# A filter layer and an ELU layer on one core: another opening, and a plain first unit

## The chip, the cores and the metric

The kernel runs on one core of a Trainium2 chip. The core has a matrix engine (PE, with its weight loads PEld), a vector engine (DVE), a scalar engine (ACT), a general one (POOL), a sequencer that issues transfers (SP), and 16 DMA engines that all transfer queues share. SP, ACT and POOL each have a queue; SP's is called q1 in the profile, ACT's q10 and POOL's q0. The metric is device time in microseconds; lower is better. The runs of a kernel spread by about 0.2%.

## What is computed

```python
X = np.fft.rfft(x, axis=1)                 # x: 8 x 3008 x 256
F = (filt_r + 1j * filt_i)[None, :, :]     # 1505 x 256 each
y = np.fft.irfft(X * F, n=3008, axis=1)
h = y.reshape(24064, 256) @ w_in           # 256 x 2048
g = np.where(h > 0, h, np.exp(np.minimum(h, 0)) - 1)
out = g @ w_out                            # 2048 x 256
```

x and the filter are float32. The two weight matrices arrive as float64: `setup_inputs` multiplies them by a float64 scalar. So the kernel has to convert them, 2 x 524288 numbers, before it can use them.

## The kernel before

**Items and quarters.** The output tokens of a batch are cut into 6 units (b, m); a unit has 4 quarters of the hidden width. Quarter q of a unit is one item. PE's order is written out by hand at the end of the kernel: item i interleaves the up steps of item i (`up_steps`, L616: y times a block of w_in, then the ELU) with the down steps of item i - 1 (`down_steps`, L703: g times a block of w_out, summed in PSUM over the four quarters). Up and down both use a seven-product scheme for the 2 x 2 blocks in place of eight products: `w_sums` forms sums of weight blocks, `n_sums` sums of y, and the products feed one another through ACT and DVE. Each step is two matmuls of 128 x 128 by 256 columns (224 in units with m = 0). All other work is hung into this order by a plan: `at(quad, place, fn)` puts a call at a place of item number quad. Numbers below zero are the time ahead of the first item.

**The transform.** 3008 = 47 x 64. For batches 1 to 7, `x_load` reads 4 rows of each half, `a_unit` multiplies with a cosine and sine table, the result goes through DRAM (`z_write`, `z_read`), then `b_unit`, `filtered` (the filter) and `bi_unit`, again through DRAM (`y_write`, `y_read`), and `n_unit` makes the y that an item uses. These steps of batch b + 1 lie between the items of batch b.

**The opening.** Batch 0 can't be hidden behind items, and the weights must be converted, so both share the stretch ahead of the first item, inside the pool "boot":

- `x_load_first` (L300) reads piece c of x, six pieces of two halves each, and a table of the full width `tf`, all on SP. The upper half is 64 rows of 4 KB, the lower half is read in mirrored order, 1 KB at a time.
- `a_first` (L310) is the first matrix step, eight matmuls a piece; ACT copies its PSUM into `zt` (L322).
- `t_first` (L325) transposes a group g of eight (L334), ACT copies (L335). `b_first` (L388) does the second matrix step (L379) and the four products with the filter on DVE (`products`, L383 to L386); `bi_first` (L402) the way back (also L379, ACT copies L411, L412); `y_write_first` writes y to DRAM. `bi_first` runs two groups behind `b_first`.
- The filter is rearranged first by 28 transfers from DRAM to DRAM on POOL (`f_arrange`, L859), then read into `ff` by 16 more (`f_read_first`, L366). Later `f_pairs` (L878) makes a second layout for the other batches, from the rearranged copy.
- The 16 weight pieces k (w_in and w_out, two each for each of the four quarters) are fetched by `w_fetch` (L787) on POOL or SP, and converted in three parts: `w_split` (two masks on DVE, L815, L816), `w_float` (four ACT steps, L825: low word, high mantissa, exponent twice), `w_join` (sign L831, sum L833, product L840 or L846, on DVE). `w_sums` (L857) follows. The temporaries sit in tiles that are idle in the opening.

Pieces 0 to 11 are converted ahead of the first item, 12 to 15 within the first four items. A DMA of the SP queue may wait for the eighth DMA before it, and so on POOL.

Of the kernel before, what the change touches and what calls it, by code (L numbers as in the profile page):

```python
# [23 lines left out]
N1 = 47  # L24
N2 = 64
NF = N // 2 + 1
P = 128
# [14 lines left out]
def _make_tables():  # L42
# [27 lines left out]
    tf = np.ascontiguousarray(ta.reshape(P, H, 4, K2).transpose(0, 1, 3, 2)).reshape(P, H, P)  # L70
# [51 lines left out]
    tw = np.ascontiguousarray(tn[:, 0:8].reshape(4, K2, 8, 2, 2, 32).transpose(1, 0, 2, 4, 3, 5)).reshape(P, 8, P)  # L122
# [19 lines left out]
def kernel(  # L142
# [47 lines left out]
    edges = glob.tile([P, 2], FP32, name="edges")  # L190
    unit = glob.tile([P, P], FP32, name="unit")
    fd = fdp.tile([NG, 2, 48, 2, 2, D], FP32, name="fd")
# [107 lines left out]
    def x_load_first(c):  # L300
        t = xs[0, c]
        u = 1 if c == 0 else 0
        nc.sync.dma_start(t[HALVES[0]].rearrange("p u d -> p (u d)"), raw(x, XC * c, [[N1 * D, 64], [1, XC * D]]))
        nc.sync.dma_start(t[HALVES[1], u:XC, :], raw(x, N1 - XC * c - u, [[N1 * D, 64], [-D, XC - u], [1, D]]))
        if c < 2:
            nc.sync.dma_start(tas[0, c], tf_d[:, 4 * c:4 * c + 4, :])
        elif c % 2 == 0:
            nc.sync.dma_start(tas.pop(("pair", c // 2)), tf_d[:, 4 * c:4 * c + 8, :])
# [16 lines left out]
    def t_first(g):  # L325

        t = t2s[0, g] = t4p.tile([P, 4, D], FP32, tag="t4", name="tf") if g % 4 > 1 else t2[:, g % 4]
        for j in range(2):
            i = j + 2 * (g % 2 if g < 4 else 0)
            ps = psO.tile([P, 2, 256], FP32, tag="po%d" % i, name="po%d" % i)  # L330
            for u in range(2):
                k = 4 * g + 2 * j + u
                for dh in range(2):
                    nc.tensor.transpose(ps[0:ROWS, u, ts(dh, P)], zt[k // 16][dh][:, ts(k % 16, ROWS)], eye)  # L334
            nc.scalar.activation(out=t[0:ROWS, 2 * j:2 * j + 2, :], in_=ps[0:ROWS], func=AXT.Copy)  # L335
# [30 lines left out]
    def f_read_first(g, t):  # L366
        for a, r in enumerate((LO, HI)):
            nc.gpsimd.dma_start(t[r].rearrange("p c u d -> p (c u d)"), fd[g, a].rearrange("q c u d -> q (c u d)"))
# [12 lines left out]
    def products(re, im, f, sr, si, p, q):  # L381

        nc.vector.tensor_tensor(out=sr, in0=re, in1=f[:, 0], op=ALU.mult)  # L383
        nc.vector.tensor_tensor(out=si, in0=re, in1=f[:, 1], op=ALU.mult)
        nc.vector.scalar_tensor_tensor(out=p, in0=im, scalar=-1.0, in1=f[:, 1], op0=ALU.mult, op1=ALU.mult)
        nc.vector.tensor_tensor(out=q, in0=im, in1=f[:, 0], op=ALU.mult)  # L386
# [15 lines left out]
    def bi_first(g):  # L402
        s = ss.pop((0, g))
        t = t3s[0, g] = (t2 if g > 5 else t3f)[:, g % 2]

        pa, pb = (psO.tile([P, 2, 256], FP32, tag="po%d" % i, name="po%d" % i)
                  for i in ((0, 1) if g > 2 and g % 2 else (2, 3)))
        for o, table, sv in ((0, gr, s[0]), (64, gi, s[1])):
            for ps, k in ((pa, LO), (pb, HI)):
                tile_mm(ps[o:o + 64], table, k, sv, g == 0 and k == LO)  # L410
        nc.scalar.activation(out=t[:, 0:2, :], in_=pa, func=AXT.Copy)  # L411
        nc.scalar.activation(out=t[:, 2:4, :], in_=pb, func=AXT.Copy)  # L412
# [113 lines left out]
    def y_read(b, m, *parts):  # L526
        t = t4s[b, m] = t4p.tile([P, 4, D], FP32, tag="t4", name="t4")
        for k in parts or (slice(0, K2),):
            if whole(b, m):
                r = slice(4 * k.start, 4 * k.stop)  # L530
                nc.sync.dma_start(t[r], yds[b].rearrange("k (p i) d -> (k p) i d", p=4)[r, 4 * m:4 * m + 4, :])
                continue
            for r in range(2):
                o = 64 * r
                nc.sync.dma_start(t[o + 2 * k.start:o + 2 * k.stop].rearrange("q i d -> q (i d)"),
                                  yds[b][k.start + r:k.stop:2].rearrange("k (p i) d -> k p (i d)", p=4)
                                  [:, :, 4 * m * D:4 * m * D + 4 * D])
# [9 lines left out]
    def n_whole(b, m):  # L547
# [10 lines left out]
        b11, b12, b21, b22 = rows  # L558
        t = yp.tile([P, 2, 256], FP32, tag="yb", name="yb")[:, :, 0:h]
# [55 lines left out]

    def up_steps(b, m, q):  # L616

# [85 lines left out]
    def down_steps(b, m, q):  # L703
        h = half(m)
# [82 lines left out]
    def w_fetch(k, queue=nc.gpsimd):  # L787
        q, j = divmod(k, 4)

        if k in (3, 4, 14, 15):  # L790
            wd = t2[:, k % 11 - 3].rearrange("p u d -> p (u d)")
        elif k == 10:
            wd = t1p.tile([P, XC, D], FP32, tag="t1", name="wd").rearrange("p u d -> p (u d)")
        elif k in (6, 7, 8, 9):
            wd = xp.tile([P, 2, 2, D], FP32, tag="xc", name="wd").rearrange("p k u d -> p (k u d)")
        else:
            wd = fbufs[{5: 0, 11: 0, 12: 1, 13: 2}.get(k, k)].rearrange("p c u d -> p (c u d)")
# [14 lines left out]
    def w_split(k):  # L812
        m, e, f, l = wts[k] = wtmp[{9: 2, 10: 1, 11: 0, 12: 3, 13: 4, 15: 5}.get(k, k % 2)]
# [4 lines left out]
    def w_float(k, *parts):  # L818
        m, e, f, l = wts[k]
        ef = e.bitcast(FP32)  # L820
        steps = ((l, wds[k][:, :, 0], AXT.Identity, 2.0 ** -52, 0.0), (f, m, AXT.Identity, 2.0 ** -20, 1.0),
                 (ef, e, AXT.Relu, -8.0, edges[:, 0:1]), (e, ef, AXT.Relu, -1.0, edges[:, 1:2]))
        for i in parts or range(4):
# [3 lines left out]
    def w_join(k, parts=(0, 1)):  # L827
        q, j = divmod(k, 4)
        m, e, f, l = wts[k]
        if 0 in parts:  # L830
            nc.vector.scalar_tensor_tensor(out=e, in0=wds.pop(k)[:, :, 1], scalar=0x80000000, in1=e,  # L831
                                           op0=ALU.bitwise_and, op1=ALU.bitwise_or)
            nc.vector.tensor_tensor(out=f, in0=f, in1=l, op=ALU.add)  # L833
        if 1 not in parts:
            return
        e = e.bitcast(FP32)
# [10 lines left out]
        if j % 2 == 1 and k < 7:  # L847
            w_sums(k)
# [10 lines left out]
    def f_arrange():  # L859

        for c, src in enumerate((filt_r, filt_i)):
            for a in range(2):
                nc.gpsimd.dma_start(fd[:, a, 0:48:2, c, :, :].rearrange("g q u d -> q g (u d)"),
                                    raw(src, 2 * a, [[64 * D, 24], [4 * D, NG], [1, 2 * D]]))
                for u in range(2):
                    g0 = 1 if a == u == 0 else 0
                    for j, n in ((0, 16), (16, 7)):
                        nc.gpsimd.dma_start(fd[g0:NG, a, 1 + 2 * j:2 * (j + n):2, c, u, :].rearrange("g q d -> q g d"),
                                            raw(src, 64 * (j + 1) - 4 * g0 - 2 * a - u,
                                                [[64 * D, n], [-4 * D, NG - g0], [1, D]]))  # L870

                g0 = 0 if a else 1
                nc.gpsimd.dma_start(fd[g0:NG, a, 47, c, :, :].rearrange("g u d -> g (u d)"),
                                    raw(src, 4, [[2 * D, NG - g0], [1, 2 * D]]))
            nc.gpsimd.dma_start(fd[0, 0, 1:48:2, c, 0, :], raw(src, 32, [[64 * D, 24], [1, D]]))
            nc.gpsimd.dma_start(fd[0, 0, 47:48, c, 1, :], raw(src, 4, [[D, 1], [1, D]]))

    def f_pairs(c, u):  # L878

        src = fd.rearrange("g a q c u d -> (g a) q c u d")[:, :, c, u, :]  # L880
        dst = fp.rearrange("g (a u) k c h d -> (g a) u k c h d", u=2)[:, u, :, c, :, :]
        nc.sync.dma_start(dst[:, :, 0, :], src[:, 0:48:2, :])
# [273 lines left out]
```

## Time and profile before

| | us |
|---|---|
| median of 3 runs | 2547.76 (2545.4 to 2550.08) |
| the profiled execution | 2546.68 |
| its span, first to last instruction | 2544.9 |
| first transpose L334 starts | 43.98 |
| first product with the filter L383 starts | 49.74 |
| last product with the filter L386 ends | 75.07 |
| first up product L631 starts | 87.57 |
| first up product of the second unit starts | 136.79 |

The mean granted clock of PE is 0.997. A busy share is an average over the span; in the opening each stage has its own limit, so it is read by stage. The chain of waits goes back from the last instruction to what released it. A float32 matmul leaves two MATMUL records, a transpose one. The length of one record is longer than the distance to the next, since matmuls and DVE or ACT instructions overlap at their ends; where work stands back to back, the distance from start to start is what it costs.

### The profile page before, as it was taken

To read this page: it belongs to the slowest core of one execution; us is meant where nothing else is said; L and a number is where in the kernel's file an instruction comes from. 1 tells how busy PE (TensorE), PEld (TensorE's weight loads), DVE (VectorE), ACT (ScalarE), POOL (GpSimd) and SP (SyncE) were. 2 spreads that over 40 slices of the span, in tenths; PEclk is the share of its full clock that TensorE was granted. 3 is DMA by queue.
4 is the path that set the end of the run, shared out by engine and by line. 5 is a ranking of instruction groups with operands and counts; after the bars stand their busy time and mean duration, and the time that the engine had idled before them with its cause. 6 is when DMAs were issued, how large, how long until landed. Compare 5 with 4: busy or idle time off the path is not lost.

```text
span 2544.9 us, 45370 instructions
## 1 busy us (share of the span) xinstructions
PE 2507.5 (99%) x17266; PEld 2158.4 (85%) x17266; DVE 2119.8 (83%) x3649; ACT 1524.0 (60%) x2680; POOL 156.9 (6%) x315
## 2 busy tenths in 40 slices
PE   6999999999999999999999999999999999999999
PEld 4788889888898888988889888888889888898887
DVE  6978888888888988889888898788897888876766
ACT  6766556655565555665555655656655665555554
POOL 5000100010000000000000000000010001000000
PEclk9999999999999999999999999999999999999999
DMA  9662213523234222342224321343213322111010
GB/s 282 184 182 59 69 39 80 135 59 70 48 93 108 63 67 50 103 97 69 49 52 131 82 67 36 84 110 82 57 48 92 85 51 69 41 41 29 9 28 17
DMA packets 229453, 198.36 MB, mean 78 GB/s; under 512 B 128326, under 2 KB 201558, under 8 KB 229236
## 3 DMA queue, kind: packets, MB, share of 16 engines
q1 hardware_dynamic: 214740, 164.57, 26.4%
q0 software_dynamic: 14000, 30.44, 4.4%
q8 instruction: 136, 2.23, 0.4%
q14 instruction: 81, 0.66, 0.1%
q10 hardware_dynamic: 496, 0.46, 0.1%
HBM read 123.50 MB, written 78.12 MB: 79 GB/s over the span
## 4 chain that ended last, share of the span: by engine, by line
PE 96%; DMA 2%; DVE 1%; ACT 1%; issue 0%; SPq 0%; ACTq 0%; DVEq 0%
PE po L715 45%; PE phs L631 25%; PE phd L631 13%; PE pha L631 6%; PE psn L580 2%; PE pf L434 1%; PE pv L501 1%; DMA xc<-in_x_dram 1%; PE psa L253 1%; PE po L379 1%; DMA x<-in_x_dram 0%; PE po L334 0%; PE psr L379 0%; PE psa L272 0%; DVE g L639 0%
## 5 line engine op out<-in xcount | busy, mean ns | idle before, releaser
L715 PE MATMUL po<-g,wo 128*128 128x256 f32 (+1 forms) x5376 | 1318.5, 377 | 0.0
L715 PEld LDWEIGHTS po<-g,wo 128*128 128x128 f32 x5376 | 1011.9, 190 | 166.0 <-issue 52.4
L642 ACT ACTIVATE g<-phs 128x512 f32<-128x512 f32 (+1 forms) x576 | 338.7, 588 | 749.4 <-PE phs L631 749.2
L649 ACT ACTIVATE e<-e 128x512 f32<-128x512 f32 (+1 forms) x768 | 477.4, 622 | 24.4
L639 DVE TENSOR_TENSOR g<-phd,g 128x512 f32<-128x512 f32 (+1 forms) x384 | 259.4, 676 | 194.4 <-ACT e L649 115.7
L653 DVE SCALAR_TENSOR_TENSOR g<-e,g 128x512 f32<-128x512 f32 (+1 forms) x576 | 387.8, 673 | 14.5 <-ACT e L649 14.4
L631 PE MATMUL phs<-y,wi 128*128 128x256 f32 (+1 forms) x1536 | 387.5, 375 | 0.4 <-ACT y L555 0.4
L631 PE MATMUL phd<-y,wi 128*128 128x256 f32 (+1 forms) x1504 | 379.7, 375 | 0.4 <-DVE g L639 0.4
L648 ACT ACTIVATE e<-g 128x512 f32<-128x512 f32 (+1 forms) x576 | 354.0, 615 | 36.8 <-DVE g L639 29.4
L631 PEld LDWEIGHTS phs<-y,wi 128*128 128x128 f32 x1536 | 291.4, 190 | 33.9 <-ACT y L555 0.6
L631 PEld LDWEIGHTS phd<-y,wi 128*128 128x128 f32 x1504 | 285.2, 190 | 33.7 <-DVE g L639 0.8
L653 DVE SCALAR_TENSOR_TENSOR g<-e,phs 128x512 f32<-128x512 f32 (+1 forms) x192 | 129.8, 676 | 88.4 <-ACT e L649 88.4
L631 PE MATMUL phs<-yt,wi 128*128 128x256 f32 (+1 forms) x768 | 193.9, 375 | 0.9 <-ACT g L642 0.9
L631 PE MATMUL phs<-yb,wi 128*128 128x256 f32 (+1 forms) x768 | 193.8, 375 | 0.6 <-ACT g L642 0.6
L631 PE MATMUL pha<-yb,wi 128*128 128x256 f32 (+1 forms) x736 | 185.9, 375 | 0.0
L648 ACT ACTIVATE e<-phs 128x512 f32<-128x512 f32 (+1 forms) x192 | 112.3, 585 | 116.5 <-PE phs L631 116.5
L373 POOL DMA_DIRECT2D fall<-fp x224 | 110.5, 501 | 822.0 <-DVE r L478 796.4
L631 PEld LDWEIGHTS phs<-yt,wi 128*128 128x128 f32 x768 | 145.7, 190 | 18.0 <-ACT g L642 1.5
L631 PEld LDWEIGHTS phs<-yb,wi 128*128 128x128 f32 x768 | 143.4, 190 | 19.9 <-ACT g L642 1.0
L639 DVE TENSOR_TENSOR g<-pha,g 128x512 f32<-128x512 f32 (+1 forms) x192 | 129.4, 674 | 32.8 <-PE pha L631 32.7
L631 PEld LDWEIGHTS pha<-yb,wi 128*128 128x128 f32 x736 | 139.8, 190 | 16.1
L692 DVE TENSOR_TENSOR g<-g,g 128x512 f32<-128x512 f32 (+1 forms) x192 | 130.7, 681 | 6.7
(190 smaller groups left out, 2067.8 us busy)
## 6 DMA issues: line engine op xcount, KB each, us to landing
yd<-t SPq DMA_DIRECT2D x127, 192.0 KB
t<-yd SPq DMA_DIRECT2D x92, 256.0 KB
fall<-fp POOLq DMA_DIRECT2D x224, 96.0 KB, 2.9
t<-z SPq DMA_DIRECT2D x224, 96.0 KB
out_dram<-o SPq DMA_DIRECT2D x624, 32.0 KB
z<-t SPq DMA_DIRECT2D x144, 128.0 KB
xc<-in_x_dram SPq DMA_DIRECT2D x84, 128.0 KB
xc<-in_x_dram SPq DMA_DIRECT2D x161, 64.0 KB
```

Source lines behind the costliest of these rows:

```text
L253: nc.tensor.matmul(ps[k][1][a:a + 32, u, :], w[r, u, 32 * o:32 * o + 32], parts[o][r, u, :], start=True, stop=True, tile_position=(32 * k, a))
L373: nc.gpsimd.dma_start(t[32 * a:32 * a + 24].rearrange("p c u d -> p (c u d)"), fp[g, a].rearrange("q c u d -> q (c u d)"))
L379: nc.tensor.matmul(ps[:, u:u + w, :], table[k, v, :], r[k, u:u + w, :], start=n == 0, stop=n == len(rhs) - 1)
L580: nc.tensor.matmul(o, t[r, i - 4 * m, ds(dh * P + 64 * c, 64)], w[r, i - 4 * m, :], start=True, stop=True)
L631: nc.tensor.matmul(ps[:, a, 0:h], w_in[q][:, COMBO[n], a, :], y[n], start=start and a == 0, stop=True, skip_group_check=True)
L639: nc.vector.tensor_tensor(out=g[o], in0=i0, in1=i1, op=ALU.add)
L642: nc.scalar.activation(out=g[o], in_=i0, func=AXT.Copy)
L648: nc.scalar.activation(out=e, in_=src, func=AXT.Relu, scale=-1.0)
L649: nc.scalar.activation(out=e, in_=e, func=AXT.Exp, scale=-1.0)
L653: nc.vector.scalar_tensor_tensor(out=g[n], in0=es[n], scalar=1.0, in1=src, op0=ALU.subtract, op1=ALU.max)
L692: nc.vector.tensor_tensor(out=b12, in0=b22, in1=b12, op=ALU.subtract)
L715: nc.tensor.matmul(po[i][:, u, 0:h], w_out[q][:, COMBO[n], a, :], g[n][:, a, :], start=q == 0 and a == 0 and n in (1, 3, 6, 4), stop=True, ...
```

## The change

Five things change, all in the opening and in the first unit (0, 0).

- **x on two queues.** The upper halves of x go on SP, the lower ones on POOL, all twelve transfers at the head of the queues. The table is half as wide (`tf` keeps two of four columns); a new `a_table(c)` spreads it by one copy and two products with a column of signs on DVE. Memsets move: the four of `zt` from POOL to DVE. PE gets warm-up matmuls ahead of and between the pieces.
- **The filter goes straight into SBUF.** `f_first(a, k, parts, queue)` replaces `f_arrange` and `f_read_first`. It fills `ff`, now laid out by frequency, in two halves (k = 0 and 8), mirrored rows on SP, straight and short ones on POOL. `f_pairs` reads the filter itself.
- **`t_first` by plain matmuls** of 64 x 64 blocks with the unit matrix instead of transposes.
- **Plain first unit.** For unit (0, 0) the steps are eight plain block products up and eight down; n_sums isn't called, and no sums of weights are needed until the second unit. These sums move to POOL, at items 1 to 5.
- **Weights piecewise.** `w_float` has three steps (the high mantissa is scaled in the sum on DVE). Pieces 0 to 5 and 7 are converted ahead of the first item; the other nine, cut into split, first and second half of the join, go between the exponential and the maximum of single blocks of items 0 to 3. The lower y writes of groups 0 to 6 go on POOL. Reads of x for batch 1 move from the end of the opening to item 2, and its x_unit, a_unit and z_write come one item later.

The core of the diff:

```diff
-    def x_load_first(c):
+    def x_load_first(c, h):
         t = xs[0, c]
+        if h == 0:
+            nc.sync.dma_start(t[HALVES[0]].rearrange("p u d -> p (u d)"), raw(x, XC * c, [[N1 * D, 64], [1, XC * D]]))
+            return
         u = 1 if c == 0 else 0
-        nc.sync.dma_start(t[HALVES[0]].rearrange("p u d -> p (u d)"), raw(x, XC * c, [[N1 * D, 64], [1, XC * D]]))
-        nc.sync.dma_start(t[HALVES[1], u:XC, :], raw(x, N1 - XC * c - u, [[N1 * D, 64], [-D, XC - u], [1, D]]))
...
+        nc.gpsimd.dma_start(t[HALVES[1], u:XC, :], raw(x, N1 - XC * c - u, [[N1 * D, 64], [-D, XC - u], [1, D]]))
+    def a_table(c):
+        t = th[:, XC * c:XC * c + XC]
+        o = tas[0, c].rearrange("p u (k f) -> p u k f", f=4)
+        nc.vector.tensor_copy(out=o[:, :, :, 0:4:2], in_=t)
+        for f, k in ((1, 1), (3, 0)):
+            nc.vector.tensor_scalar(out=o[:, :, :, f], in0=t[:, :, :, k], scalar1=signs, scalar2=None, op0=ALU.mult)
...
+        for k in range(4):
+            for dh in range(2):
+                for o, n in ((0, 64), (64, ROWS - 64)):
+                    for r, p in zip(HALVES, ps):
+                        nc.tensor.matmul(p[o:o + n, k, dh, :], zt[k // 2][dh][r, (2 * g + k % 2) * ROWS + o:(2 * g + k % 2) * ROWS + o + n],
+                                         eye[r, r], start=True, stop=True)
...
+    def f_first(a, k, parts, queue):
+        o, row, e = 64 * a, 16 * a + k, 1 if a == k == 0 else 0
+        for c, src in enumerate((filt_r, filt_i)):
+            if "f" in parts:
+                queue.dma_start(ff[o:o + 48:2, c, k:k + 8].rearrange("q k d -> q (k d)"), raw(src, row, [[64 * D, 24], [1, 8 * D]]))
+            for j, m, part in ((0, 16, "m"), (16, 7, "s")):
+                if part in parts:
+                    r = o + 1 + 2 * j
+                    queue.dma_start(ff[r:r + 2 * m:2, c, k + e:k + 8], raw(src, 64 * (j + 1) - row - e, [[64 * D, m], [-D, 8 - e], [1, D]]))
...
+    def plain_ups(b, m, q):
...
+        def step(i, j, k):
+            if k == 0:
+                held[i, j] = bank("php")
+            n, ps = held[i, j]
+            for a in range(2):
+                nc.tensor.matmul(ps[:, a, 0:h], w_in[q][:, 2 * k + i, a, :], rows[k][j],
+                                 start=k == a == 0, stop=True, skip_group_check=True)
+            if k == 1:
+                src = ps[:, :, 0:h]
+                e = ep.tile([P, 2, 256], FP32, tag="e", name="e")[:, :, 0:h]
+                nc.scalar.activation(out=e, in_=src, func=AXT.Relu, scale=-1.0)
+                nc.scalar.activation(out=e, in_=e, func=AXT.Exp, scale=-1.0)
+                for fn, a in plan.get((q, 7, i, j), ()):
+                    fn(*a)
+                nc.vector.scalar_tensor_tensor(out=g[i, j], in0=e, scalar=1.0, in1=src, op0=ALU.subtract, op1=ALU.max)
+                banks.append(held.pop((i, j))[0])
+                for fn, a in plan.get((q, 8, i, j), ()):
+                    fn(*a)
...
+            for c in range(NXC):
+                x_load_first(c, 0)
+                x_load_first(c, 1)
+                if c == 0:
+                    nc.gpsimd.dma_start(flat_th[:, 2 * XC:H], tf_d[:, 2 * XC:H])
+            nc.sync.dma_start(once, once_d)
+            w_fetch(0)
+            for k in range(0, 16, 8):
+                for parts, queue in (("m", nc.sync), ("f", nc.gpsimd), ("s", nc.gpsimd)):
+                    for a in range(2):
+                        f_first(a, k, parts, queue)
+                if k == 0:
+                    nc.sync.dma_start(gs, gs_d)
+                    w_fetch(1)
...
+            for c in range(NXC):
+                a_table(c)
+            for c in range(NXC):
+                a_first(c)
+                if c < NXC - 1:
+                    warm(1, 256)
+            for g in range(2):
+                t_first(g)
+            step(0)
+            for g in range(2, 4):
+                t_first(g)
+            w_join(0)
...
+        rest = (8, 6, 9, 10, 11, 12, 13, 14, 15)
+        line = []
+        for n, k in enumerate(rest):
+            line += [(k2, "s") for k2 in rest[n + 1:n + 2]] + [(k, "a"), (k, "b")]
...
+        for quad, *counts in ((0, 1, 1, 1, 1, 1, 1, 1, 0), (1, 1, 1, 1, 1, 1, 1, 1, 1), (2, 1, 1, 1, 1, 1, 1, 1, 1), (3, 1, 1, 1, 0, 0, 0, 0, 0)):
+            for n, count in enumerate(counts):
+                plan.setdefault((quad, 7 + n % 2, *BLOCKS[n // 2]), []).append((convert, (count,)))
```

## The prediction

> **What bounds the kernel now.** The totals and the forty slices come first. PE is busy 99% of the span; the one slice below 9 is the first, and it is also the one in which POOL works and in which the transfers run at 9 tenths of their engines.
>
> ```profile
> span 2544.9 us, 45370 instructions
> PE 2507.5 (99%) x17266; PEld 2158.4 (85%) x17266; DVE 2119.8 (83%) x3649; ACT 1524.0 (60%) x2680; POOL 156.9 (6%) x315
> ...
> PE   6999999999999999999999999999999999999999
> ...
> DMA  9662213523234222342224321343213322111010
> ```
>
> So every change of PE's work after the opening counts in full, and an earlier start of that work counts in full too. Next the chain of waits of the first 90 us: in time order, start, length, what.
>
> ```profile
> 3.20 12.56 DMA xc<-in_x_dram
> 15.78 12.88 DMA xc<-in_x_dram
> 28.68 11.88 DMA x<-in_x_dram
> 40.69 3.46 PE psa L315 x16
> 44.70 3.57 PE po L334 x31
> ```
>
> Until 40.6 the opening hangs on the pieces of x, and on nothing PE does. Third, busy time by stage (columns: PE, PEld, DVE, ACT, POOL, then PE's granted clock, DMA share, GB/s). I cut at the first transpose L334, the end of the filter step, the first up product L631, and the first of the second unit.
>
> ```profile
> 0.00:43.98 43.98, 19.14 (x97) 18.15 (x97) 26.24 (x53) 29.16 (x52) 22.34 (x45) 0.88 1.00 307
> 43.98:76.98 33.00, 32.54 (x270) 18.34 (x268) 27.10 (x50) 25.03 (x47) 11.38 (x20) 1.00 0.94 235
> 76.98:87.57 10.59, 8.30 (x31) 4.44 (x30) 9.49 (x23) 10.00 (x18) 0.00 (x0) 1.00 0.79 238
> 87.57:136.79 49.22, 45.41 (x281) 41.25 (x282) 45.82 (x88) 36.01 (x65) 0.52 (x1) 1.00 0.60 161
> ```
>
> Stage 1 (44 us) is bound by bytes: DMA share 1.00. Stage 2 (33) is shared by PE and DVE. Stage 3 (10.6) is the trip of y through DRAM. Stage 4 is the first unit. The waits of the same stretch show what holds the start of the products:
>
> ```profile
> PE psa L315 <- DMA tn<-tf_t: 16.4, 2, 14.7
> ...
> DVE rq L383 <- DMA ff<-fd: 3.4, 1, 3.4
> ```
>
> **Stage 1, x first.** Before, the queues carry, ahead of the last piece of x, weights 0 to 6, 1.5 MB of table and the filters' copy through DRAM: 44 us at 307 GB/s. After, ahead of it stand on SP a third of the half table and six upper halves, on POOL six lower halves and the rest of the table; the filters, `once` and weight 0 follow. The queues share the engines. In the stretch 6 to 14 us the two rows are:
>
> ```profile
> q0 software_dynamic: 480, 1.54, 66.1%
> q1 hardware_dynamic: 504, 0.79, 36.2%
> ```
>
> Equal counts of packets, not of bytes, though one has 3.2 KB packets and the other 1.6. So POOL's 1600 packets up to its last piece of x (192 + 5 x 256 of 1 KB, 128 of 4 KB) let about 1600 of SP pass: 128 of 2 KB, 384 + 256 of 4 KB (x, two weights), 128 of 1.5 KB, some 700 of 1 KB (`once`, mirrored filters). A packet of about 1.1 KB costs 74 ns of an engine (88 to 94 us: 1030 in 79.6% of 96 engine-us), one of 3.4 KB 196 ns (2 to 6 us: 225 in 69% of 64), so 4 KB about 210, an estimate. Sum 2176 x 0.074 + 768 x 0.21 + 27 = 349 engine-us, over 16 and the overlapped share of 1.04: 21 us. From 3.2 it lands at 24.2. Bounds: only x and table (3.9 MB at 307 GB/s) 16; 60 packets per us of POOL as in 6 to 14, 30. I take 24.2, by rows of just this competition.
>
> Per piece PE needs 2.0 us (L315 x16 at 23.84) and one warm matmul, 0.4: hidden but for the last. The 18 DVE steps that spread the half table (0.3 to 0.4 us each by the 0.42 of L815, estimate 5.5 us in all) come after a 3.5 us memset and end near 13, ahead of the pieces; without that cover they would cost their 0.9 us a piece. The first t_first starts at 24.2 + 2.0 + 0.7 (copies L322) = 26.9, against 43.98.
>
> **Stage 2.** t_first turns one group with 64 records of 64x64 form, where before it took 8 transposes. The nearest row of that form is L580 x128 in 2.05 us, so 1.03 per group, against 1.02 of L334 x8: no gain, no loss. But on ACT weight 0's conversion (3 steps, 0.57 + 0.73 + 0.73 start to start) now stands behind two groups' copies (4 x 0.5), and on DVE its join (three steps, 0.60, 0.60, 0.72 as L831, L833, L840) before the first product: copies end 30.0, float 32.0, join 2.0, first product 34.0, where before it was 49.74 (after the 3.41 wait for `ff`). The filter no longer goes through DRAM: 44 transfers (28 of L863 to L876, 16 of L368) become 26 that write `ff` directly. Its first half, 14 of them behind x on two queues, lands near 29.5 (POOL's last two wait for two slots, then 0.6 us of issue and about 3 to land): covered by 4 us; the second near 34, not needed before 46. From first product to last end: 8 x 4 x 0.60 = 19.2, three splits 2.0, one join 2.0, PE waits 1.5 (before 2.3): 24.7, end 58.7 (before 75.07). POOL now issues seven of the eight lower y writes; 0.6 us each with 3 us between, nothing queued behind waits.
>
> **Stage 3** keeps its length: from the last product 12.5 us to the first up product: 71.2 against 87.57, a gain of 16.3. DVE must do five joins and six splits in it, 5 x 2.0 + 6 x 0.67 = 14, done 1.5 us after that, just ahead of the first g. Bounds 10 to 22 by x alone (at 30 and 18).
>
> **Stage 4, plain first unit.** Eight up and eight down steps a quarter for seven: 8 more steps of 0.757 (L631 from 107.86 to 108.62): +6.06, on PE, certain. Saved on DVE: the four L592 sums, and per quarter some Strassen sums, not on the path. Before, 49 steps (37.1), one psn (1.8) and two psa (3.8) fill 42.7 of the 49.2 us: 6.5 us of stall, the longest behind DVE (1.67 and 0.60 before L631 phd). I let them go, as plain blocks don't feed each other, and the two psa move behind the unit with their own cover. What is late next: nine conversions (8, 6, 9 to 15) go between exp and max of the blocks. ACT has per block 1.12, per conversion 2.03 (one step of 0.62 fewer than before) and, as its exponent steps wait for a split queued behind a max on DVE, 0.65 more: 16 x 1.12 + 9 x 2.68 + 1.1 = 43 us for 56 steps (42.4): even. In order: in the second quarter PE waits for a bank 1.5; weight 13 is joined 37.6 us after the first up product and wanted at 35.2, 2.4; at the unit's end two ACT copies of `po` hold the next down, 0.8 (before they lay under the last steps); x_unit and a_unit of batch 1 come a quad later, which leaves one quad (12.1 us) for psa copies, four z writes (3.5), landing 3.0, reads 1.6 + 2.7, 0.9 ahead: 11.7, so 0.3. The read of y for the second unit now stands on SP behind ten weight transfers; 5.25 MB at some 290 GB/s (82 to 88 us) put it 13 us after the first up product, wanted at 18: covered, by 5 us. Sum 5.0; bounds 0 (all even out) and 11 (each twice over). POOL's 32 sums (L857 0.73 each, 23 us) run beside; they're needed from the fourth quarter on. The pairs' copies now read the filters themselves, and later reads of yd are cut in four for two: SP's issue time, off the path.
>
> **Sum.** -16.3 + 6.06 - 6.5 + 5.0 = -11.7 on the profiled execution's 2546.68 (span 2544.9), which lies 1.1 below the median shown: 2535 by it, 2536 as a median. A measurement of this kernel tells no change from one within 0.2%, 5.1 us.
>
> **Rivals.** (a) x comes sooner, as if bytes alone counted (18 us): 6 us less, 2530. For: the share sometimes exceeds 1.08. Against: the equal packets. (b) x on two queues comes hardly sooner than 30, or PE starts stage 2 at a low clock: before, an idle stretch (25.9 to 30.1) is followed by a granted clock of 0.63 to 0.69 until 45. After, the gap between the first two pieces is about 3.3 us. Price: the last piece 3.46 for 2.0 and some 3 us of stage 2: 2541; with x at 30, 2542. The Trainium skill, "TensorE: Matmul & The Clock Gate", Part 1, has an idle window of about 3.4 us halve the clock, and a busy one restore it; the trace's fall after 4.3 us idle agrees, its 15 us of return doesn't.
> (c) POOL can't issue while DVE works. Before, POOL's issues at 2.4 to 5.3 us lie under the 3.47 us memset of `ff` and take 0.55 as others, against it. If the memsets (1.2 to 6.5) held POOL, its pieces would start 5 us later, partly made up as SP would be done: +4, 2540. The Trainium skill, "SBUF — State Buffer", "SBUF: two separate sides", says that POOL's queue starves under a two-port DVE copy; the six copies of the half table are such, and no run here shows them yet.
> (d) Slower: the conversions pace the first unit. Their 0.65 us hand-over is worked out, not seen; ACT and DVE are in order, so a block's max waits behind a split that waits for a temp, and the temp for a join. It decides when a hand-over costs 1.3 us more in each of nine (11.7); at 2.5 more (22) the time is 2558. For it: ACT has no slack (43 of 42.4). Against: DVE has (about 9 of 12 us a quarter), and four banks let PE run one quarter ahead.
>
> **How the numbers follow.** Forecast 0.52; (a) 0.15; (b) 0.12; (c) 0.08; (d) 0.13. Faster: 0.52 + 0.15, most of (b) and (c): 0.80; within 0.2%: 0.08; slower 0.12. Range 2525 (x at 16 and three of the five us of stall gone) to 2548 (x at 30 and stall 11, or the start of d); without d the forecast's own is 2529 to 2543.
>
> **What would show it.** Last x piece near 24; first t_first near 27 (before 43.98); first product near 34, waiting for weight 0's join and not for `ff`; first up product near 71; 56 steps in some 49 us; no DVE wait of PE before them above 2 us. Wrong if x lands near 30, if the products wait for `ff`, or if PE waits in the first unit add up to 12 us or more.

## The result, and the profile after

The changed kernel takes 2558.1 us (median; 2552.4 to 2560.3), the kernel before 2547.6 (2545.4 to 2550.1) beside it: a ratio of 1.0038, 95% interval 1.0025 to 1.0051. The forecast was 2536, faster. The change costs 10.5 us where 11.7 were to be won.

The profiled execution of the changed kernel is the shortest of its six, 2552.35 us; the other five took 2557 to 2560. So the trace below accounts for 5.7 us of loss against the profiled execution of before, and the rest has to be found elsewhere (the first experiment). Its head, totals and two rows of slices:

```profile
span 2550.5 us, 46325 instructions
...
PE 2520.4 (99%) x17766; PEld 2167.4 (85%) x17766; DVE 2105.0 (83%) x3607; ACT 1509.4 (59%) x2652; POOL 173.0 (7%) x325
...
PE   7899999999999999999999999999999999999999
...
DMA  8653213512234232342224321343223322111010
```

PE is as full as before, its second slice excepted (64 to 127 us), which was 9 before and is 8 now. The stages, cut at the first record of the turn L346, the end of the last copies of the filter step, the first up product L663 and the first of the second unit L730 (busy time of PE, PEld, DVE, ACT, POOL, then PE's granted clock, DMA share, GB/s):

```profile
0.00:23.65 23.65, 18.88 (x114) 14.80 (x114) 9.24 (x29) 12.14 (x24) 10.09 (x20) 1.00 0.94 238
23.65:71.97 48.32, 38.01 (x719) 23.92 (x719) 29.25 (x50) 24.22 (x44) 13.14 (x23) 0.89 0.72 184
71.97:81.32 9.35, 8.46 (x32) 4.36 (x31) 9.07 (x18) 7.87 (x13) 1.09 (x2) 1.00 0.77 232
81.32:136.46 55.14, 49.23 (x276) 46.20 (x277) 47.33 (x78) 37.84 (x66) 23.56 (x26) 1.00 0.53 175
```

Stage 1 is done 20 us sooner than before, 3 sooner than forecast. Stage 2 takes 48.3 us where it took 33.0, and PE is busy for 38 of them. The first up product comes at 81.3: of the 16.3 us that were to be gained, 6.25 are left. The first unit takes 55.1 us, about 6 more than the 49 forecast for its 56 steps. At the second unit's first product, 136.46 against 136.79, only 0.3 is left of the gain.

The chain of waits shows the opening (start, length, what):

```profile
2.10 8.87 DMA t<-tf_t
12.83 2.02 PE psa L322 x16
...
21.94 1.80 PE psa L322 x16
28.93 5.84 issue
40.73 2.71 issue
```

Where the chain of before hung on the pieces of x until 40.6, this one hangs on the table `tf` until 11, and from 12.8 to 23.7 on PE's own work on the pieces of x, 2.2 us each, of which 0.43 is a warm-up matmul. PE waits for no piece of x there. Then the chain holds two pieces called "issue": PE stands still and waits for nothing that the profile shows. The waits of 23 to 72 us (engine, line, waited for: total, times, longest) say what these do:

```profile
PE po L346 <- issue: 9.1, 3, 5.8
...
DVE rq L407 <- PE po L402: 7.0, 3, 4.8
DVE rq L407 <- PE psi L402: 5.9, 2, 5.4
```

The products wait for PE now, 5.4 us before the first and 4.8 before the third, where before they waited 3.4 for `ff`. No product waits for `ff` any more. PE in the first unit, and in the 54 us behind it:

```profile
PE php L663 <- DVE g L672: 4.9, 4, 1.9
PE php L663 <- DVE wi L947: 1.0, 1, 1.0
```

```profile
PE phd L730 <- DVE g L738: 2.0, 1, 2.0
```

So there are three places to explain: PE without work in the turn, DVE late in the first unit, DVE late once more behind it.

### The profile page after: what moved, and what is told of

It reads as the page before. It is cut to its first block, busy times and chain, and to the rows that moved or that the text cites. A ratio compares the mean times of both kernels' runs of the same rounds, so it can differ in the third digit from the quotient of the medians.

```text
span 2550.5 us, 46325 instructions
## 1 busy us (share of the span) xinstructions
PE 2520.4 (99%) x17766; PEld 2167.4 (85%) x17766; DVE 2105.0 (83%) x3607; ACT 1509.4 (59%) x2652; POOL 173.0 (7%) x325
## 4 chain that ended last, share of the span: by engine, by line
PE 95%; DVE 2%; DMA 1%; issue 1%; ACT 1%; SPq 1%; POOL 0%; ACTq 0%; DVEq 0%; POOLq 0%
PE po L816 44%; PE phs L730 25%; PE phd L730 12%; PE pha L730 6%; PE psn L608 2%; PE pf L458 1%; PE pv L525 1%; PE psa L254 1%; PE po L402 1%; PE po L690 0%; SPq L866 0%; PE po L346 0%; PE psa L322 0%; DMA t<-tf_t 0%; PE psr L402 0%
## 5 line engine op out<-in xcount | busy, mean ns | idle before, releaser
L816 PE MATMUL po<-g,wo 128*128 128x256 f32 (+1 forms) x5264 | 1293.8, 377 | 0.0
L816 PEld LDWEIGHTS po<-g,wo 128*128 128x128 f32 x5264 | 990.8, 190 | 165.3 <-issue 51.7
L741 ACT ACTIVATE g<-phs 128x512 f32<-128x512 f32 (+1 forms) x564 | 332.2, 589 | 743.4 <-PE phs L730 743.3
L748 ACT ACTIVATE e<-e 128x512 f32<-128x512 f32 (+1 forms) x752 | 468.1, 623 | 23.9
L752 DVE SCALAR_TENSOR_TENSOR g<-e,g 128x512 f32<-128x512 f32 (+1 forms) x564 | 380.2, 674 | 14.2 <-ACT e L748 14.1
L730 PE MATMUL phs<-y,wi 128*128 128x256 f32 (+1 forms) x1504 | 380.0, 375 | 0.0
L730 PE MATMUL phd<-y,wi 128*128 128x256 f32 (+1 forms) x1488 | 376.0, 375 | 0.4 <-DVE g L738 0.4
L747 ACT ACTIVATE e<-g 128x512 f32<-128x512 f32 (+1 forms) x564 | 347.1, 615 | 36.0 <-DVE g L738 29.2
L730 PEld LDWEIGHTS phs<-y,wi 128*128 128x128 f32 x1504 | 285.6, 190 | 33.0
L730 PEld LDWEIGHTS phd<-y,wi 128*128 128x128 f32 x1488 | 282.2, 190 | 33.7 <-DVE g L738 0.8
L730 PE MATMUL phs<-yb,wi 128*128 128x256 f32 (+1 forms) x752 | 190.2, 375 | 0.3 <-ACT g L741 0.3
L730 PE MATMUL phs<-yt,wi 128*128 128x256 f32 (+1 forms) x752 | 190.0, 375 | 0.0
L730 PE MATMUL pha<-yb,wi 128*128 128x256 f32 (+1 forms) x736 | 185.9, 375 | 0.0
L730 PEld LDWEIGHTS phs<-yb,wi 128*128 128x128 f32 x752 | 140.4, 190 | 19.6 <-ACT g L741 0.7
L730 PEld LDWEIGHTS phs<-yt,wi 128*128 128x128 f32 x752 | 142.8, 190 | 16.5
L730 PEld LDWEIGHTS pha<-yb,wi 128*128 128x128 f32 x736 | 139.8, 190 | 16.1
```

Of the source, the lines that this page charges most:

```text
L730: nc.tensor.matmul(ps[:, a, 0:h], w_in[q][:, COMBO[n], a, :], y[n], start=start and a == 0, stop=True, skip_group_check=True)
L741: nc.scalar.activation(out=g[o], in_=i0, func=AXT.Copy)
L747: nc.scalar.activation(out=e, in_=src, func=AXT.Relu, scale=-1.0)
L748: nc.scalar.activation(out=e, in_=e, func=AXT.Exp, scale=-1.0)
L752: nc.vector.scalar_tensor_tensor(out=g[n], in0=es[n], scalar=1.0, in1=src, op0=ALU.subtract, op1=ALU.max)
L816: nc.tensor.matmul(po[i][:, u, 0:h], w_out[q][:, COMBO[n], a, :], g[n][:, a, :], start=q == 0 and a == 0 and n in (1, 3, 6, 4), stop=True, ...
```

## The experiments

**A second profile of the changed kernel.** No edit.

> The changed kernel unchanged, for a second profile: its profiled execution (2552.35 us, mean granted clock 0.998) was the shortest of its six, the other five took 2557 to 2560 at a mean clock of 0.995. 0.003 of 2556 us is 7.7 us of PE clock. If PE's two empty stretches in the turn (5.84 and 2.71 us that wait for nothing the profile shows) and the half clock behind them make this spread, a profile of a longer execution has its extra 5 to 6 us between 24 and 70 us, at a granted clock of 0.5. If the spread comes from elsewhere (the first unit, the end), the opening is the same to 1 us in both.

2557.54 us, span 2555.8. The two empty stretches are 6.38 us (from 28.42) and 4.28 us (from 40.01). The first up product comes at 83.99, 2.7 us later; the first unit takes 55.97, 0.8 more; behind it 1.7 more are lost. The expectation was half right: half of the extra time lies in the opening, not all. The empty stretches themselves are 2.1 us longer. The rest is visible in the granted clock. By the clock records of the trace it is 0.50 in the profile shown above from 32.94 to 39.77 and from 43.18 to 46.59; in this one from 31.40 to 38.23, from 45.05 to 51.88, from 113.32 to 116.73 and from 167.93 to 171.35. These lengths are 6.83 and 3.41, and 6.83, 6.83, 3.41 and 3.42: one or two times 3.41 us. The falls of one execution also lie whole multiples of it apart: 31.40 and 45.05 four, 31.40 and 167.93 forty. The Trainium skill ("TensorE: Matmul & The Clock Gate", Part 1) has the clock decided in free-running windows of 3413 ns; the trace agrees. The two late windows lie in the first unit and behind it, where the 0.8 and the 1.7 are lost. So an execution differs from the next by how long its stalls are and by how many windows they catch.

**The turn by transposes.** In `t_first`, the changed kernel otherwise as it is:

```
-        for k in range(4):
-            for dh in range(2):
-                for o, n in ((0, 64), (64, ROWS - 64)):
-                    for r, p in zip(HALVES, ps):
-                        nc.tensor.matmul(p[o:o + n, k, dh, :], zt[k // 2][dh][r, ...], eye[r, r], start=True, stop=True)
+        for j in range(2):
+            ps = psO.tile([P, 2, 256], FP32, tag="po%d" % i, name="po%d" % i)
+            for u in range(2):
+                for dh in range(2):
+                    nc.tensor.transpose(ps[0:ROWS, u, ts(dh, P)], zt[j][dh][:, ts(2 * g + u, ROWS)], eye)
```

> The changed kernel with the turn t_first done by 8 transposes a group again instead of 32 matmuls, all else the same: 1024 instructions of PE fewer (64 records a group become 8, each with its weight load). Theory A, PE runs out of instructions: the q8 packets of 16 KB land at 22-24, 32-34, 40-42 and 44-46 us in the changed kernel, one just ahead of each restart of PE. Then the empty stretches go, the first product comes about 32.5 (when weight 0 is joined) instead of 37.5, the last ends about 58 instead of 69, the first up product comes about 70 instead of 81.3, and the time falls by 11 to 17 us from 2558: 2541 to 2547. Theory B, something else in that stretch holds PE (the landing of zt, the copies on ACT, the saturated DMA engines as such): the stretches stay, 2555 to 2560.

The edit takes away 896 instructions of PE, not 1024: 448 matmul records (17766 to 17318) and as many weight loads. The result is 2541.6 us (2539.7 to 2548.9), ratio to before 0.9985 (0.9976 to 0.9994): 16.5 us under the changed kernel, and now under the kernel before. No wait for "issue" is left in the turn. The first product follows at once on the join of weight 0 (DVE, start, length):

```profile
29.95 0.69 DVE L943 TENSOR_TENSOR wi<-wme 128x512 f32<-128x512 f32 x1
30.56 0.68 DVE L403 TENSOR_TENSOR rq<-psr,ff 128x512 f32<-128x512 f32 x1
```

In the changed kernel it came at 37.49. The last product starts at 55.56 instead of 68.67, the first up product at 68.19 instead of 81.32. The first unit is what it was, 55.16 us. So the trace puts 13.1 us into the turn, all that the edit touches. The medians differ by 16.5; these two profiles don't show the rest. That PE ran out of instructions is not yet shown by it: form, data path and number of the matmuls all changed at once. The end of this section settles that.

**The sums later.** POOL's sums of the weights, one list of places changed:

```
-((1, 2, 1), (2, 2, 3), (2, 0, 5), (3, 2, 7), (3, 0, 9), (4, 2, 11), (4, 0, 13), (5, 2, 15))
+((3, 0, 1), (3, 0, 3), (4, 2, 5), (4, 0, 7), (5, 2, 9), (5, 0, 11), (6, 2, 13), (6, 0, 15))
```

> The changed kernel with POOL's sums of the weights moved later: those of quarter 0 to quad 3, 1 to quad 4, 2 to quad 5, 3 to quad 6, just ahead of their first use, out of the conversions. Theory A, a sum on POOL lengthens the step of DVE beside it (0.94 for 0.42 of L914 and L915, 1.22 for 0.68 of L929): DVE's conversion steps in the first unit return to their own length, PE's waits for DVE there fall from 5.9 us to about 2, and the time falls by 2 to 4: 2554 to 2556. Theory B, the hand-overs between ACT and DVE alone pace the first unit: the waits stay at 5 to 6 and the time within 1 us of 2558.

> Transposes in the turn and the sums late, both together. If both theories A hold and add up: 13 to 20 us under the changed kernel, 2538 to 2545, so 3 to 9 us under the kernel before (2547.6). If the conversions still pace the first unit once it starts earlier (their last weights land no earlier, at 94 us), part of the 11 us comes back as waits for weights in quarters 2 to 4, and the time is 2545 to 2550.

Neither gained. Alone the edit gives 2561.9 us (four executions, 2554.0 to 2564.1), which is not clear of the changed kernel's spread. With the transposes it gives 2548.3 (2546.7 to 2549.7), 6.6 above the transposes alone. The edit didn't do what it was to do. A place in the program's order is no place in time on an engine that waits for nothing else: POOL ran ahead of PE and did the sums in one go, still among the conversions (POOL's timeline of the run with both edits):

```profile
89.67 3.60 POOL L958 TENSOR_TENSOR wi<-wi 128x256 f32<-128x256 f32 x4
93.23 3.71 POOL L958 TENSOR_TENSOR wo<-wo 128x256 f32<-128x256 f32 x4
96.91 3.51 POOL L958 TENSOR_TENSOR wi<-wi 128x256 f32<-128x256 f32 x4
100.37 4.06 POOL L958 TENSOR_TENSOR wo<-wo 128x256 f32<-128x256 f32 x4
```

Nearly every step of DVE between 90.6 and 101.5 is lengthened there, the joins are late, and PE waits 4.1 us for joined weights (L943) where it waited 1.0 with the transposes alone; the first unit takes 58.60 us instead of 55.16. PE's wait behind the unit grows too, from 2.2 to 4.4. As a test of theory A this is inconclusive in its own terms; crowded together, the same sums cost more, which speaks for it.

**The sums on DVE.** On the kernel with the transposes:

```
-        for quad, place, k in ((1, 2, 1), (2, 2, 3), (2, 0, 5), (3, 2, 7), ...):
-            at(quad, place, w_sums, k, nc.gpsimd)
+        for quad, place, k in ((3, 0, 1), (3, 1, 3), (4, 2, 5), (4, 1, 7), (5, 2, 9), (5, 1, 11), (6, 2, 13), (6, 1, 15)):
+            at(quad, place, w_sums, k)
```

> e1 (transposes in the turn), and the sums of the weights on DVE instead of POOL, at places that DVE's own order keeps: quarter 0 in quad 3, 1 in quad 4, 2 in quad 5, 3 in quad 6, so none beside a conversion. POOL computes nothing in the first unit. Theory A, the sums on POOL lengthen DVE's steps: of the conversion steps from 70 to 125 us none is longer than its own length (0.42, 0.68, 0.68), PE's waits in the first unit fall from 6.4 us to 2 to 3, and the time by 2 to 4 us under e1's 2541.6: 2538 to 2540; the 32 sums of 0.42 us are 11 to 13 us of DVE in quads 3 to 6 and hidden, as DVE is busy 59 of 84 us there. Theory B, ACT's and DVE's hand-overs pace the first unit whatever POOL does: its waits stay at 6 and the time at 2541 to 2543. If DVE has no room in quads 3 to 6, PE waits there instead: 2543 to 2548.

2538.5 us (2536.3 to 2547.4), ratio 0.9972 (0.9960 to 0.9984), and the first unit takes 50.88 us instead of 55.16. PE's waits in it fall from 5.9 to 2.3. (The 6.4 of the expectation had in it a wait of 0.5 ahead of the unit.) The interval of the median overlaps that of the transposes alone, so the trace has to carry theory A, and it shows it step by step. Here are steps of two conversions in the changed kernel, on DVE, beside POOL's sums of 94.73 to 97.4 and 104.66 to 107.1:

```profile
95.85 0.94 DVE L914 TENSOR_SCALAR wme<-wd 128x512 uint32<-128x512 uint32 x1
96.72 0.94 DVE L915 TENSOR_SCALAR wme<-wd 128x512 uint32<-128x512 uint32 x1
...
106.47 1.22 DVE L929 SCALAR_TENSOR_TENSOR we<-wd,we 128x512 uint32<-128x512 uint32 x1
```

The same steps where POOL is silent (the run that follows the next, whose first unit takes 50.88 too):

```profile
88.58 0.42 DVE L910 TENSOR_SCALAR wme<-wd 128x512 uint32<-128x512 uint32 x1
88.91 0.42 DVE L911 TENSOR_SCALAR wme<-wd 128x512 uint32<-128x512 uint32 x1
89.25 0.68 DVE L925 SCALAR_TENSOR_TENSOR we<-wd,we 128x512 uint32<-128x512 uint32 x1
```

POOL pays as well (nanoseconds, smallest, median, largest, in the changed kernel):

```profile
L962 POOL TENSOR_TENSOR wi<-wi x16: 729/852/1182, 70.7 to 131.3; 128x256 f32<-128x256 f32 x16
```

A sum of 0.73 us that meets a step of DVE adds some 0.5 to most of these steps, as in the lines above. DVE is busy for 47.33 us of the first unit with the sums on POOL, and for 41.63 with them on DVE, though eight of the sums are in it then (8 x 0.42 = 3.3): 9.0 us of DVE's time in the first unit was lengthening. The sixteen steps of L672, which have one operand in PSUM, stay between 0.607 and 0.622 throughout. The Trainium skill ("SBUF — State Buffer", "SBUF: two separate sides") calls the pair of ports that POOL and DVE share an exclusive lock for the whole instruction, for steps of DVE with two operands in SBUF or in its two-port mode; what is lengthened here and what isn't agrees with that.

**The third unit's table product later.** On the kernel with the transposes, the one collision behind the first unit:

```
                     if b == 0 and m == 2:
-                        s = 29
+                        s = 30
...
-                        at(t + quad, place, n_sums, b, m, *parts)
+                        at(t + quad + ((b, m) == (0, 2)), place, n_sums, b, m, *parts)
```

> e1, and the third unit's table product, its sums and its reads one quad later (quads 6 and 4 instead of 5 and 3), so that they do not stand on DVE with the steps of x_unit, which the change moved into quad 5. Theory: PE's one wait after the first unit (phd for g, 2.2 us in e1) is this collision: it goes, and the time falls by 2 us to 2539.6. Rival: the wait is for x itself, which arrives late; then it stays, 2541 to 2542.

2541.1 us (2537.7 to 2547.4), ratio 0.9972 (0.9961 to 0.9983): the median moves by 0.5 us, the shortest execution by 2.0. PE's wait of 2.2 us is gone from the trace, and nothing has taken its place but 0.4 for z. That x wasn't late is seen in the changed kernel's DVE, where everything stands in one line behind the third unit's copy:

```profile
159.22 0.69 DVE L636 SCALAR_TENSOR_TENSOR yb<-y,y 128x512 f32<-128x512 f32 x1 [5.78 <-ACT y L613]
...
162.34 0.69 DVE L239 TENSOR_TENSOR xc<-xc 128x512 f32<-128x512 f32 x1
162.94 0.69 DVE L738 TENSOR_TENSOR g<-phd,g 128x512 f32<-128x512 f32 x1
```

The two sums of the third unit and four steps of `x_unit`, 3.7 us, go ahead of the g that PE waits for. Before, `x_unit` stood a quad (an item of the plan) earlier, and PE has no wait in the 54 us behind the first unit. The chain of waits names x (a transfer of 4.66 us from 156.97) as the releaser; the run shows it was the line on DVE.

This run and the one before it also have executions that are 6 to 9 us longer than their others, and the profile of each fell on one. The sums-on-DVE run shows how (PE's clock is the third number from the end):

```profile
32.00:34.00 2.00, 0.91 (x2) 0.19 (x2) 1.75 (x3) 0.67 (x2) 0.57 (x1) 1.00 0.98 190
34.00:36.00 2.00, 1.84 (x16) 1.31 (x18) 2.00 (x5) 0.68 (x1) 0.58 (x1) 0.83 0.99 211
36.00:44.00 8.00, 8.00 (x34) 3.68 (x30) 5.84 (x10) 3.83 (x6) 2.41 (x5) 0.50 1.05 234
44.00:52.00 8.00, 7.28 (x36) 3.01 (x32) 3.15 (x6) 2.29 (x4) 1.02 (x2) 0.50 0.93 333
```

PE waits 1.10 us for a bank at 32 to 33.1, the clock halves at 35.3, and it stays there to 52.4, 17.1 us or five windows. The last product starts at 64.36. In the three runs with the transposes whose clock held it starts at 54.6 to 56.3.

**Both, on the transposes.**

> e4 and e5 together. If both theories hold: 4 to 6 us under e1, 2536 to 2538. If neither: 2541.

2535.7 us (2535.3 to 2537.6), ratio 0.9953 (0.9938 to 0.9969): below both kernels, by 22 us under the changed one and by 11 under the one before. Its totals and its first unit:

```profile
span 2533.9 us, 45416 instructions
...
PE 2518.9 (99%) x17318; PEld 2163.6 (85%) x17318; DVE 2105.8 (83%) x3639; ACT 1508.4 (60%) x2652; POOL 145.2 (6%) x293
```

```profile
21.84:57.88 36.04, 34.06 (x272) 18.64 (x271) 28.94 (x52) 23.59 (x44) 11.50 (x20) 1.00 0.97 252
57.88:67.22 9.34, 8.47 (x33) 4.37 (x31) 7.32 (x16) 7.88 (x14) 0.00 (x0) 1.00 0.82 240
67.22:118.10 50.88, 48.62 (x276) 46.29 (x277) 41.63 (x86) 38.04 (x66) 0.52 (x1) 1.00 0.54 176
```

Stage 2 has 272 records of PE instead of 719 and takes 36 us instead of 48; the first unit is 4.3 us shorter.

**Idle matmuls.** What the transposes took away was tested by giving the number back without the turn. On the kernel of the last run, ahead of each group's eight transposes:

```
+        for n in range(28):
+            h, o = n % 2, 64 * (n // 2 % 2)
+            nc.tensor.matmul(ps[h][o:o + 48, 0, 0:64], eye[HALVES[h], o:o + 48], eye[HALVES[h], 0:64], start=True, stop=True)
```

> e6, and ahead of the 8 transposes of each group 28 idle matmuls in the 64x64 form of the changed kernel that multiply only the identity and whose result the transposes overwrite: 64 records of PE a group again, as in the changed kernel, but none of the turn's data goes through that form. Theory A, PE runs out of instructions because there are many: the empty stretches that wait for nothing (5.8 and 2.7 us in the changed kernel) come back at about 29 and 41 us, with the half clock behind them, and the time is 2546 to 2553. Theory B, the 64x64 form of the turn itself (its reads of zt, its eight copies) held PE: only the idle matmuls' own time is added, 8 groups of about 0.6 us, partly beside DVE: 2536 to 2541, and no wait for nothing above 0.8 us.

The second run has `range(28 if g > 3 else 0)`.

> The same idle matmuls in groups 4 to 7 alone, which lie 2.4 to 3 us apart among the products, 28 x 4 matmuls more in all. If what counts is a burst (256 records within 5 us, groups 0 to 3), instructions keep up here: no empty stretch, 2536 to 2539. If they cannot be fetched faster than some 16 KB in 10 us at this load whatever their spacing, an empty stretch of 2 to 5 us shows between 38 and 48 us: 2539 to 2546.

In all groups: 2552.2 us (2544.4 to 2555.9), 16.5 above the kernel without them, ratio to before 1.0013 (1.0002 to 1.0025). In groups 4 to 7 alone: 2539.2 (2538.3 to 2541.0), ratio 0.9962 (0.9950 to 0.9974). The empty stretch is back, in its old place, with matmuls that nobody needs (PE's timeline of the first):

```profile
35.03 0.68 PE L344 MATMUL po<-once 64*48 64x64 f32 x16 [5.10 <-issue]
```

Its clock is 0.50 from 34.1 to 40.9 behind it. The second stretch stayed small here, 0.32 us. In the second run there is no wait for "issue" in the turn, and its 3.5 us are about what the idle matmuls take themselves (54 records in 0.99 us, four groups). The idle matmuls have the form of the turn, so this pair of runs doesn't part the form from the number. The queue that carries instructions does. In the changed kernel it moves one packet in each of 22 to 24, 32 to 34, 40 to 42 and 44 to 46 us, so one ahead of each restart; all queues from 32 to 34:

```profile
q0 software_dynamic: 55, 0.28, 58.2%
q1 hardware_dynamic: 108, 0.15, 36.1%
q8 instruction: 1, 0.02, 4.2%
```

Where PE stops settles it. Counted in the traces (matmuls, weight loads, and the waits of the sequencer), PE has begun 705 instructions when the first empty stretch comes and 961 when the second comes, 256 more. It is 705 and 961 in the changed kernel, in its second profile, in the run with the sums later alone, and again with the idle matmuls. Each time PE starts again 1.35 to 1.70 us after the end of the packet: in the changed kernel at 34.77 after 33.36 and at 43.43 after 42.08. So PE had come to the end of a block of 256 instructions and waited for the next block. The whole traces agree. The changed kernel's 35871 instructions of PE are 140.1 such blocks; its packets, and those with the transposes, are:

```profile
q8 instruction: 140, 2.29, 0.4%
```

```profile
q8 instruction: 136, 2.23, 0.4%
```

The Trainium skill ("Runtime: NRT & Kernel Launch", "Instruction fetch mechanics") has code come in blocks of 16 KiB, 256 instructions: the trace agrees. The page also has the fetch mostly hidden behind the issue of instructions; here it isn't, and 5.84 us is the measure.

With the idle matmuls in groups 4 to 7 alone, the packets are there 5.9 and 4.2 us before PE comes to the same two ends, although the DMA share is 1.05 from 38 to 46 us. So full queues alone make no empty stretch; PE must also use up a block fast. What sets how late a packet comes is open. In the four traces with long stretches, the two packets start 5.7 to 7.0 us after PE began the block before, at a DMA share of about 1.0, and the next one 1.1 to 3.8 us after, at 0.7 to 0.8. That x, weights and filters delayed the packets was not tried: no edit makes these transfers wait without moving the work that needs them.

## Why the prediction was wrong

*Stage 1, x first: the time nearly, the path not.* The first t_first came at 23.65, forecast 26.9. The forecast had the last piece of x at 24.2, with PE's work hidden but for that piece. By the trace the last lower half landed at 19.59, nearer to the 18 of rival (a) (when the upper halves landed is not told). PE began the second piece at 12.83, when its lower half had just landed (12.74), and then worked without a pause, 2.2 us a piece, so PE's work on five pieces ended the stage, and the four warm-up matmuls (0.43 each) lay in its path. That the time is only 3 us off is partly luck. Rival (c) is out: POOL had issued all its pieces by 5.8, under DVE's memset. The filters' first half is never waited for, as forecast.

*Stage 2: the step that failed.* It read: "The nearest row of that form is L580 x128 in 2.05 us, so 1.03 per group, against 1.02 of L334 x8: no gain, no loss." The duration is right (64 records in 1 us), and it is not the price. Eight instructions of work became 64, each with its weight load, and 256 of them stand in a row, at a time when every queue is full. The row taken as the nearest is a single burst of 128 records in a quiet stretch (DMA share 0.00 from 201.0 to 203.2). The price is two empty stretches of 8.6 us together, the half clock behind them, and the first and third product late by 5.4 and 4.8: the last product ends at 69.35 instead of 58.7. With the transposes it ends at 56.24, 25.7 after the first product's start; the 24.7 for products, split, join and PE's waits stood. By the run with the transposes the step costs 13.1 us of the profiles and 16.5 of the medians. Of the 13.1, PE's waits for "issue" are 9.1, and the half clock while PE works some 4.1 (half of 8.2 us). That the idle matmuls cost 16.5 too is chance: of their 16.1 at the last product, some 8 is the time that eight groups of them take themselves (0.99 each), 5.4 the empty stretches, and 2.9 the half clock.

Rival (b) had the half clock, but from a gap between pieces of x; it came from the empty stretches. With it a stall of 9.1 us became a loss of 13.1 at the first up product of the profiled executions (81.32 against 68.19) and of 16.5 in the median, and the changed kernel's executions differ by 8 us. One reading behind this rival was wrong: the 15 us at 0.63 to 0.69 before are an average. By its clock records that clock was 0.50 from 30.02 to 33.44 and from 36.85 to 43.68 and full between, with a second idle stretch of 2.26 us from 33.7. So it came back after one window and after two.

*Stage 3: right.* 11.97 us from the last product's end to the first up product, forecast 12.5; with the transposes 11.95.

*Stage 4, plain unit.* The 6.06 for eight more steps was worked out, not isolated by a run. It fits: in the kernel with both edits the unit takes 50.88 with 2.3 of waits, before 49.22 with 3.8 and one `a_unit` (1.9 to 2.4) more; without these the work grew by 5.1 to 5.6, and seven of the eight steps lie in the unit, 5.3. The 6.5 us of stall that the forecast let go was the remainder of a sum; PE's waits in that unit before add up to 3.8.

*The sums on POOL: the second step that failed.* "POOL's 32 sums (L857 0.73 each, 23 us) run beside." They were costed at nothing, with DVE's slack as the cover in (d). They took 9.0 us of that slack, and that cost 4.3 us on PE. The 0.65 for a hand-over between ACT and DVE was right where POOL is silent: ACT waits 4.4 us in seven for the split there, 0.63 each. Beside POOL's sums it is 9.4 us in seven, 1.34 each. Rival (d) gave 2558 and the time is 2558, but for another reason: the conversions lengthened the first unit by 4.3, not by 22.

*x_unit a quad later: the third, and small.* The 0.3 was worked out from x, z and the copies alone. What stands in the quad that it was moved into was not read: there the third unit's sums lie in the same queue. PE's wait is 2.0 to 2.5 in the traces; the run without it moved the median by 0.5, so what it costs is not settled.

*The sum.* On the profiled execution 2552.35 - 2535 = 17.4: 10.1 from stage 2 and the start, 6.1 from the first unit, some 1.7 behind it (the wait of 2.0 less the 0.3), less 0.5 that is not placed. The median lies 5.8 above that; in the second profile, 5.2 longer, 2.7 of it is in the opening and 2.5 in the two late windows of the clock. The kernel without the three costs takes 2535.7; that this is the forecast of 2536 to a fraction is partly luck, as stage 1 ended 3 us sooner for another reason, the stall let go was too large, and the clock has a part in every median.

## What to carry to other kernels

Count instructions as well as microseconds: a step rewritten into eight times as many small matmuls needs the row of a burst as long, under the same load, before it is called even. An engine "beside" another is free only if no step of the other is longer for it: compare the smallest and the largest duration of one form, with and without the neighbour. Where work moves to a later place, read what already stands in that place's queue; and where it moves in the order of an engine that waits for little, it doesn't move in time.

## What the runs showed of the hardware that was not expected

PE stood still for 5.84, 6.38 and 5.10 us, each time after 705 instructions, until 1.4 to 1.7 us after the next 256 had come in as one packet of 16 KB. Some 208 to 232 records of the small matmuls within 5 to 7 us, each with its weight load, were enough, at a DMA share of 1.0.

The granted clock fell to 0.50 after waits as short as 1.10 us (sums on DVE, at 32 us) and 1.41 (third unit later, at 32.4), and not after 0.25 at the same place (both edits) nor after 1.12 at 27 us (idle matmuls in groups 4 to 7). The Trainium skill ("TensorE: Matmul & The Clock Gate", Part 1) wants an idle window of some 3.4 us for it; here there was none, so the measurement decides. Cut into the windows of 3.41 us that the falls mark, the eleven traces (the first 15 us and the end left out) have 22 falls. Of these, 18 follow a window in which PE was idle for 1.87 us or more, and only one window with as much (1.89) had no fall. The other four follow 0.36 to 1.55 us, while many windows with 1.2 to 1.77 had no fall; what sets these four apart was not found. The clock stayed low for one, two, three or five windows (3.4, 6.8, 10.2, 17.1 us) with PE busy by the profile for most of them; what decides how long was not found either.

One tensor_tensor of POOL, 128x256 in 0.73 us, lengthened most steps of DVE that it met, by up to some 0.54 us (0.42 to 0.94, 0.68 to 1.22), and was itself lengthened to as much as 1.18.
